# A fused attention and two mixture-of-experts layers on one core: x kept in weight slots, work reordered, products padded to fewer shapes

## The chip, the cores and the metric

One core of a Trainium2 chip. The time is the device time of one execution in microseconds; lower is better. Three executions are given with their median. A further execution was recorded by the profiler: its span runs from the first to the last instruction, and its own time is a little longer than the span.

## The reference, cut to what matters

Three layers run one after another. The attention has batch 4, 8 heads, 576 positions and 64 dimensions a head, and adds two parts.

```python
q_d, k_d, v_d = (z.reshape(B, H, S // 4, 4, D).mean(3) for z in (q, k, v))
out_up = repeat(softmax_attention(q_d, k_d, v_d), 4)     # pooled part
mask = abs(i - j) < 4                                    # banded part
x = out_up + softmax_attention(q, k, v, where=mask)      # then rows (2304, 512)

logits = x @ w_gate                                      # first expert layer
# the largest of all 2304 x 8 logits first: each token goes to one expert, each expert takes 288
out[mask_e] = relu(x[mask_e] @ w1[e]) @ w2[e]

logits = x @ phi                                         # second layer, 8 experts x 4 slots
d = softmax over tokens, c = softmax over slots
slot_out[e] = relu((d.T @ x)[e] @ m2w1[e]) @ m2w2[e]
out = c @ slot_out
```

## The kernel before, in words

The attention works in eight units, each two batches and two heads: the rows of a unit's arrays hold two heads, the columns two batches. Per unit the arrays loaded are k (64 rows x 1152 columns twice), q (128 x 1152), v (112 x 2304, cut into overlapping strips), and vp (128 x 1024 and 64 x 512, v grouped for pooling), all of 4 bytes, 2.87 MB. `load_k`, `load_q`, `load_v` and `load_p` (L68 to L89) issue them on SP; k, q and vp have two buffers, v has three.

Each step of a unit is a small function. For the banded part: `l_scores` (products of 32 queries with 38 keys, behind one product that writes the mask), `l_max`, `l_exp`, `l_norm`, `l_tr` (transposes on TensorE; ScalarE copies them into `aT`, and the ninth tile into `a8`), `l_av` (products with v; the ninth tile's contract 38 rows, the others 102). For the pooled part: `pool_k`, `pool_q`, `pool_v` on GpSimd, `d_scores`, `d_max`, `d_exp`, `d_norm`, `d_tr` (L220, transposes and small products of `e` and `e2`), `d_tr_out`, `d_av` (L252), `d_out`. `l_add` sums both into `xT`, x transposed; `l_x` (L305) transposes three row tiles at a time into `xu` (two buffers), and `l_st` (L322) stores a unit's 128 columns of x for nine row tiles into `x_dram` from ScalarE's queue: 0.59 MB in pieces of 512 bytes. `l_logit` adds the gate's logits.

The order is written out by hand. `FIRST` lists the steps before the first period, `UNIT0` those of period 0, `UNIT` those of the periods 1 to 8; an entry is a step and the unit relative to the period, so in period u the scores of unit u+1, the products with v of unit u and x of unit u-1 are made, and unit u+2 is loaded. Each engine, and SP's queue too, takes its instructions in this order.

Weights come through `Stream` (WS, L862): 1 MB slots, loads in the order of `todo` as slots come free. Nine slots `a0` to `a8` are there from the start. The entry `pump` loads one slot in each of the periods 2 to 6 and all free ones in period 7, when three of the attention's buffers are handed over too. After the attention eight slots `b0` to `b7` follow. The first 16 loads are halves of w2 transposed; `PMaker` (L511) makes P, the product of phi with each half, 32 TensorE products each, and `turn` transposes a finished one on VectorE.

`gating` searches prices for the eight experts in five rounds: VectorE and ScalarE compare, TensorE counts, a transposed sum goes back. Two P products stand behind the start and behind each round, one behind the totals and three behind the verdict (L788), at the end of `dispatch`. When the verdict is known, all engines branch, and `moe` starts: its rows of x are gathered by three indirect DMAs (`first_gather`), issued as soon as the indices `idx` are there.

In `moe` each expert's tokens go through `x_t` (transposes), `split` (a weight tile into two parts), `hidden` (12 products of 288 columns), `relu`, `h_rows`, the second layer's logits and weighted sums; lists give the order (`START`, `PERIOD`, `END`, `LAST`). `FINISH` lists the second layer: `first` and `second` are its products, `gathered` collects the slots' outputs, `combine` makes and stores the result. `weighted` (L1297) sums into four PSUM tiles, for the last expert named m, l, h and t; l is also read by `soft_lt`.

Of the kernel before, what the change touches and what calls it, by code (L numbers as in the profile page):

```python
# [36 lines left out]
def attention(nc, tc, ctx, kv, q, k, v, vp, C, x_dram, logit_tok, wg, pump):  # L37
# [145 lines left out]
    def d_exp(u):  # L183
# [3 lines left out]
        s["e2"] = e2 = sb.tile([64, SD, 2], F32, name="e2")  # L187
# [4 lines left out]
        for h in range(2):  # L192
            nc.scalar.activation(e2[:, :, h], p[0:64, h, 2], AF.Exp, bias=mx[0:64, h, 2:3], scale=1.0 / 128,
                                 accum_out=sm[0:64, h, 2:3])
        nc.scalar.activation(small(u, 24, 30), sm.rearrange("p h g -> p (h g)"), AF.Identity, bias=C["eps4"], scale=4.0)

    def d_norm(u):
        s = st[u]
        r = small(u, 24, 30)
        nc.vector.reciprocal(r, r)  # L200
        r = r.rearrange("p (h g) -> p g h", h=2)
        for bi in range(2):
            nc.vector.tensor_mul(s["e"][:, bi], s["e"][:, bi], r[:, bi, None, :].to_broadcast([128, SD, 2]))
        nc.vector.tensor_mul(s["e2"], s["e2"], r[0:64, 2, None, :].to_broadcast([64, SD, 2]))

    def l_tr(u, g):
        s = st[u]
        if g == 2:
            s["a8"] = sb.tile([128, 128], F32, name="a8")
# [3 lines left out]
        n = (3, 3, 2)[g]  # L213
        for r in range(2):
            sl = slice(64 * r, 64 * r + W)
            nc.scalar.activation(aT[sl, 3 * g:3 * g + n, :, r], p[sl, 0:n].rearrange("p s (c q) -> p s c q", c=4), AF.Copy)  # L216
        if g == 2:
            nc.scalar.activation(s["a8"][0:64 + W], p[0:64 + W, 2], AF.Copy)

    def d_tr(u):  # L220
# [6 lines left out]
        for h in range(2):  # L227
            nc.tensor.transpose(p[0:PD, 1, 64 * h:64 * h + 64], e2[:, 0:PD, h], ident[0:64, 0:64])
# [5 lines left out]
        for bi in range(2):  # L234
            for h in range(2):
                o, sl = slice(PR * h, PR * h + PR), slice(PR * bi, PR * bi + PR)
                c = 128 + SD * bi
                nc.tensor.matmul(p[o, 1, c + PD:c + SD], e2[:, PD:SD, h], ident[0:2 * PR, sl], start=True, stop=True,
# [13 lines left out]
    def d_av(u):  # L252
        s = st[u]
        od = tpsum([128, 2, SD])
        for bi in range(2):
            for part in range(2):
                for h in range(2):
# [3 lines left out]
                    nc.tensor.matmul(od[64 * h:64 * h + 64, bi], w, m, start=part == 0, stop=part == 1, skip_group_check=True)  # L261
# [12 lines left out]
    def l_av(u):  # L274
# [10 lines left out]
        for c in range(4):  # L285
            for h in range(2):
                rows = slice(64 * h, 64 * h + W)
                nc.tensor.matmul(p8[64 * h:64 * h + 64, QB * c:QB * c + QB], rows_v(s, rows, 8, c), s["a8"][rows, QB * c:QB * c + QB],
# [16 lines left out]
    def l_x(u, g):  # L305
        s = st[u]
        xT = s["xT"].rearrange("d b s -> d (b s)").rearrange("d (t i) -> d t i", i=128)
        p = tpsum([128, 3, 128])
        for i in range(3):
            nc.tensor.transpose(p[:, i], xT[:, 3 * g + i], ident)  # L310
        if g == 0:
            s["xu"] = sb.tile([128, 9, 128], F32, name="xu")
        nc.scalar.activation(s["xu"][:, 3 * g:3 * g + 3], p, AF.Copy)  # L313
# [20 lines left out]
    stages = dict(load_k=load_k, load_q=load_q, load_v=load_v, load_p=load_p, pool_k=pool_k, pool_q=pool_q, pool_v=pool_v,  # L334
# [23 lines left out]
    load_p(0)  # L358
    load_v(0)
# [6 lines left out]
    for t in dsm_b:  # L366
        nc.vector.memset(t, 1.0)
    edges(1)
# [10 lines left out]
FIRST = [  # L379
    ("load_k", 1),  # L380
    ("pool_k", 0, 0),
    ("load_q", 1),
    ("pool_k", 0, 1),
    ("pool_q", 0),
    ("d_scores", 0),
    ("d_max", 0),
    ("load_p", 1),
    ("d_exp", 0),
    ("l_scores", 0),
    ("load_v", 1),  # L390
    ("l_max", 0),
    ("d_norm", 0),
    ("pool_k", 1, 0),
    ("l_exp", 0),
    ("d_tr", 0),
    ("d_tr_out", 0),
    ("load_k", 2),
    ("pool_v", 0),
    ("pool_k", 1, 1),
    ("l_norm", 0),  # L400
    ("load_q", 2),
    ("l_scores", 1),
]
UNIT0 = [
    ("l_tr", 0, 0),
    ("l_tr", 0, 1),
    ("load_v", 2),
    ("pool_q", 1),
    ("d_av", 0),
    ("load_p", 2),  # L410
    ("d_out", 0),
    ("l_max", 1),
    ("d_scores", 1),
    ("d_max", 1),
    ("pool_v", 1),
    ("l_exp", 1),
    ("l_norm", 1),
    ("d_exp", 1),
    ("l_tr", 0, 2),
    ("d_norm", 1),  # L420
    ("l_av", 0),
    ("pump", 0),
    ("d_tr", 1),
    ("l_add", 0),
    ("pool_q", 2),
    ("l_x", 0, 0),
]
UNIT = [
    ("d_tr_out", 0),
    ("load_k", 2),  # L430
    ("pool_k", 1, 0),
    ("pool_k", 1, 1),
    ("load_q", 2),
    ("l_scores", 1),
    ("d_av", 0),
    ("l_tr", 0, 0),
    ("l_max", 1),
    ("load_v", 2),
    ("l_logit", -1),
    ("l_tr", 0, 1),  # L440
    ("l_exp", 1),
    ("d_scores", 1),
    ("l_tr", 0, 2),
    ("d_out", 0),
    ("d_max", 1),
    ("d_exp", 1),
    ("l_av", 0),
    ("l_add", 0),
    ("l_x", -1, 1),
    ("d_norm", 1),  # L450
    ("pool_v", 1),
    ("pool_q", 2),
    ("load_p", 2),
    ("l_x", 0, 0),
    ("l_x", -1, 2),
    ("l_norm", 1),
    ("l_lg", -1),
    ("l_st", -1),
    ("d_tr", 1),
    ("pump", 0),  # L460
# [50 lines left out]
class PMaker:  # L511
# [18 lines left out]
    def products(self, psum):  # L530
        self.product(psum)
        self.product(psum)

# [49 lines left out]
def gating(nc, tc, ctx, L, C, Z, idx, fill, first, force=None):  # L583
# [10 lines left out]
    def psum(shape):  # L594
        return ps.tile(shape, F32, name="t", bufs=4)
# [15 lines left out]
    fill.products(psum)  # L611
# [44 lines left out]
    def rounds(n, start=False):  # L656
        for r in range(n):
# [12 lines left out]
            fill.turn()  # L670
            fill.turn()
# [970 lines left out]
```

## Time and profile before

| | |
|---|---|
| three executions | 424.38, 428.37, 428.44 us, median 428.37 |
| profiled execution | 427.75 us, span 426.0 us |
| mean granted clock of TensorE | 0.917 |
| busy: TensorE, VectorE, ScalarE, GpSimd | 360.7, 235.9, 180.5, 127.4 us |
| moved by DMA | 122.52 MB, mean 288 GB/s |

Times in rows are microseconds from the span's start unless marked ns. PE is TensorE, DVE VectorE, ACT ScalarE, POOL GpSimd, SP the queue that issues most DMAs. A row of a timeline gives start, length from the first start to the last end, engine, line, operation, output and input by their names in the program, shapes and count, and in brackets the idle time ahead of it and who ended it. One product of 32-bit numbers shows as two records, a transpose as one. Idle time of an engine that does not bind costs nothing; a wait for several others is put down to the one that came last.

### The profile page before, as it was taken

To read this page: it belongs to the slowest core of one execution; us is meant where nothing else is said; L and a number is where in the kernel's file an instruction comes from. 1 tells how busy PE (TensorE), PEld (TensorE's weight loads), DVE (VectorE), ACT (ScalarE), POOL (GpSimd) and SP (SyncE) were. 2 spreads that over 40 slices of the span, in tenths; PEclk is the share of its full clock that TensorE was granted. 3 is DMA by queue.
4 is the path that set the end of the run, shared out by engine and by line. 5 is a ranking of instruction groups with operands and counts; after the bars stand their busy time and mean duration, and the time that the engine had idled before them with its cause. 6 is when DMAs were issued, how large, how long until landed. Compare 5 with 4: busy or idle time off the path is not lost. (4 is left out here: it accounts for less than half of the span.)

```text
span 426.0 us, 12313 instructions
## 1 busy us (share of the span) xinstructions
PE 360.7 (85%) x5116; PEld 270.1 (63%) x5116; DVE 235.9 (55%) x636; ACT 180.5 (42%) x497; POOL 127.4 (30%) x167
## 2 busy tenths in 40 slices
PE   0779989899559876757899999999999898689994
PEld 0456666666328556656878787887879685233693
DVE  4653647645505189763456676665758475424253
ACT  6362765567135434103545454453636343101231
POOL 6466663725340000042205050505141102240000
PEclk9885999989855899966999999999999999989997
DMA  8999978798997798934485999999997696989965
GB/s 230 274 268 246 205 201 274 226 291 264 260 397 275 226 382 310 425 109 161 157 295 195 329 333 335 353 360 323 363 321 254 230 390 267 373 320 411 408 244 217
DMA packets 31962, 122.52 MB, mean 288 GB/s; under 512 B 3232, under 2 KB 13088, under 8 KB 22688
## 3 DMA queue, kind: packets, MB, share of 16 engines
q1 hardware_dynamic: 19968, 111.85, 76.7%
q10 hardware_dynamic: 9632, 4.85, 4.1%
q0 software_dynamic: 2304, 5.02, 4.0%
q8 instruction: 41, 0.67, 0.7%
q14 instruction: 17, 0.14, 0.1%
HBM read 111.97 MB, written 9.73 MB: 286 GB/s over the span
## 5 line engine op out<-in xcount | busy, mean ns | idle before, releaser
L1293 POOL DMA_INDIRECT lg_rows<-lt,idx x24 | 24.6, 1026 | 114.0 <-DVE lt L1274 109.1
L1211 PE MATMUL h<-V,wh 128*128 128x288 f32 x128 | 37.9, 317 | 2.3 <-ACT V L1188 1.1
L1211 PE MATMUL t<-V,wh 128*128 128x288 f32 x128 | 37.9, 318 | 1.6 <-ACT wh L1196 1.6
L1212 PE MATMUL h<-V,wh 128*128 128x288 f32 x128 | 36.5, 306 | 0.5 <-DVE a L887 0.5
L1212 PE MATMUL t<-V,wh 128*128 128x288 f32 x128 | 35.0, 296 | 0.0
L216 ACT ACTIVATE aT<-t 38x384 f32<-38x384 f32 (+1 forms) x48 | 21.5, 448 | 26.4 <-PE t L212 25.6
L1198 DVE TENSOR_TENSOR wl<-b,wh 128x512 fp32r<-128x512 f32 x32 | 21.7, 682 | 18.7 <-ACT wh L1196 18.5
L1211 PEld LDWEIGHTS t<-V,wh 128*128 128x128 f32 x128 | 24.1, 188 | 8.5 <-issue 5.7
L1226 DVE STREAM_TRANSPOSE V<-hT 128x288 f32<-128x288 f32 x64 | 27.1, 453 | 4.1 <-issue 4.1
L1211 PEld LDWEIGHTS h<-V,wh 128*128 128x128 f32 x128 | 25.1, 196 | 6.4 <-issue 2.8
L1198 DVE TENSOR_TENSOR wl<-a,wh 128x512 fp32r<-128x512 f32 x32 | 21.7, 678 | 11.2 <-ACT wh L1196 10.7
L180 DVE TENSOR_REDUCE lg<-D 128x6 f32<-128x864 f32 x8 | 8.5, 1067 | 34.6 <-PE D L172 34.6
L1196 ACT ACTIVATE wh<-b 128x512 fp32r<-128x512 f32 x32 | 20.0, 631 | 16.4 <-DVEq L851 10.5
L1175 POOL DMA_INDIRECT kT<-x_dram,idx x21 | 20.2, 963 | 21.0 <-PE t L1186 17.0
L1212 PEld LDWEIGHTS h<-V,wh 128*128 128x128 f32 x128 | 25.2, 197 | 0.8 <-DVE a L887 0.8
L1220 ACT ACTIVATE hT<-h 128x288 f32<-128x288 f32 x32 | 13.1, 409 | 29.7 <-PE m L1243 15.3
L1212 PEld LDWEIGHTS t<-V,wh 128*128 128x128 f32 x128 | 24.1, 189 | 0.1
L1196 ACT ACTIVATE wh<-a 128x512 fp32r<-128x512 f32 x32 | 20.3, 633 | 8.5 <-PE h L1212 5.0
L282 PE MATMUL S<-aT,V 102*64 102x64 f32 x512 | 19.4, 239 | 5.0 <-ACT aT L216 2.9
L1214 PE MATMUL h<-V,wl 128*128 128x288 f32 x128 | 22.8, 301 | 0.0
L313 ACT ACTIVATE xu<-t 128x384 f32<-128x384 f32 x24 | 10.8, 485 | 27.9 <-DMA x_dram<-xu 17.4
L282 PEld LDWEIGHTS S<-aT,V 102*64 102x64 f32 x512 | 17.9, 152 | 7.3 <-ACT aT L216 3.1
(310 smaller groups left out, 963.5 us busy)
## 6 DMA issues: line engine op xcount, KB each, us to landing
a<-in_moe_w_dram SPq DMA_DIRECT2D x27, 1024.0 KB, 7.8
b<-in_moe_w_dram SPq DMA_DIRECT2D x21, 1024.0 KB, 12.1
a<-in_moe_w2t_dram SPq DMA_DIRECT2D x9, 1024.0 KB, 8.7
V<-in_v_dram SPq DMA_DIRECT2D x8, 1008.0 KB, 12.8
kT<-in_k_dram SPq DMA_DIRECT2D x16, 288.0 KB, 11.5
qT<-in_q_dram SPq DMA_DIRECT2D x8, 576.0 KB, 12.8
x_dram<-xu ACTq DMA_DIRECT2D x8, 576.0 KB, 13.7
vp<-in_vp_dram SPq DMA_DIRECT2D x8, 512.0 KB, 13.6
```

The costliest lines, as they stand in the source:

```text
L216: nc.scalar.activation(aT[sl, 3 * g:3 * g + n, :, r], p[sl, 0:n].rearrange("p s (c q) -> p s c q", c=4), AF.Copy)
L282: nc.tensor.matmul(p[64 * h:64 * h + 64, k // 2, o:o + 64], rows_v(s, slice(0, 64 + W), 2 * k + h, c), aT[0:64 + W, 2 * k + h, c].rearrang ...
L313: nc.scalar.activation(s["xu"][:, 3 * g:3 * g + 3], p, AF.Copy)
L1175: nc.gpsimd.indirect_dma_start(out=xs[0:96, DM * c:DM * c + DM], out_offset=None, in_=x_dram, in_offset=bass.IndirectOffsetOnAxis(ap=idx[: ...
L1196: nc.scalar.activation(wh, w, AF.Copy)
L1198: nc.vector.tensor_sub(wl, w, wh.bitcast(F32))
L1211: nc.tensor.matmul(p, wh[:, dt], xh[:, dt], start=dt == 0, stop=False)
L1212: nc.tensor.matmul(p, wh[:, dt], xl[:, dt], start=False, stop=False)
L1214: nc.tensor.matmul(p, wl[:, dt], xh[:, dt], start=False, stop=dt == 3)
L1220: nc.scalar.activation(h, st.pop(("ph", e, ft)), AF.Relu)
L1226: nc.vector.transpose(st["hb", e][:, :, ft], st.pop(("hr", e, ft)).rearrange("p (b t) -> p b t", t=32))
L1293: nc.gpsimd.indirect_dma_start(out=lg_rows[3 * e + c], out_offset=bass.IndirectOffsetOnAxis(ap=idx[:, 3 * e + c:3 * e + c + 1], axis=0), i ...
```

## The change

Eight parts.

1. x stays on the chip for four units: `l_x` makes 4 + 4 + 1 row tiles and writes them into slots `a5` to `a8` (and a small tile), and `l_st` stores all 512 columns once after units 3 and 7, from SP. `Stream` starts with five slots; `a5` and `a6` join in period 7, `a7` and `a8` behind the `b` slots.
2. Products: the ninth tile of l_av contracts 102 rows from `aT`; `e2` has 128 rows with zeros, its transposes become products of 128 rows; d_av makes its 32-row products first and its 112-row ones after.
3. `FIRST`, `UNIT0` and `UNIT` are reordered: unit 0's scores ahead of its pooled part, its vp and v loaded later.
4. `warm` products, which write a tile that nobody reads, in `FIRST`: 10, 10 and 16 of 256 bf16 columns.
5. P: three products at the gate's start, one in the last round, four behind the totals, none behind the verdict; finished ones are transposed in the rounds and behind the verdict.
6. `moe` starts with 8 + 2 + 2 warm products of 512 columns around `x_t`; `LAST` has 10.
7. `weighted` of the last expert writes m, h, h, t.
8. `FINISH`: `first_t` and, near the end, `second` and `gathered` stand earlier.

```diff
@@ attention
-    aT = one.tile([128, 8, 4, 2, QB], F32, name="aT")
+    aT = one.tile([128, 9, 4, 2, QB], F32, name="aT")
+    e2_b = [one.tile([128, SD, 2], F32, name=f"e2{i}") for i in range(2)]
...
     def l_tr(u, g):
-        if g == 2:
-            s["a8"] = sb.tile([128, 128], F32, name="a8")
...
-            nc.scalar.activation(aT[sl, 3 * g:3 * g + n, :, r], p[sl, 0:n].rearrange("p s (c q) -> p s c q", c=4), AF.Copy)
-        if g == 2:
-            nc.scalar.activation(s["a8"][0:64 + W], p[0:64 + W, 2], AF.Copy)
+            nc.scalar.activation(aT[sl, 3 * g:3 * g + 3, :, r], p[sl].rearrange("p s (c q) -> p s c q", c=4), AF.Copy)
     def d_tr(u):
...
-            nc.tensor.transpose(p[0:PD, 1, 64 * h:64 * h + 64], e2[:, 0:PD, h], ident[0:64, 0:64])
+            nc.tensor.matmul(p[0:PD, 1, 64 * h:64 * h + 64], e2[:, 0:PD, h], ident[:, 0:64], start=True, stop=True,
+                             skip_group_check=True)
...
     def d_av(u):
-        for bi in range(2):
-            for part in range(2):
+        for part in (1, 0):
+            for bi in range(2):
...
     def l_av(u):
-                rows = slice(64 * h, 64 * h + W)
-                nc.tensor.matmul(p8[...], rows_v(s, rows, 8, c), s["a8"][rows, QB * c:QB * c + QB],
+                nc.tensor.matmul(p8[...], rows_v(s, slice(0, 64 + W), 8, c), aT[0:64 + W, 8, c, h],
...
     def l_x(u, g):
+        n = (4, 4, 1)[g]
+        p = tpsum([128, n, 128])
+        for i in range(n):
+            nc.tensor.transpose(p[:, i], xT[:, 4 * g + i], ident)
+        if hp == 0:
+            if g < 2:
+                x = wa.tile([128, 2048], F32, name=f"a{5 + 2 * pr + g}").rearrange("p (t d) -> p t d", d=DM)
+            else:
+                x = sb.tile([128, 1, DM], F32, name="xu8")
+            st["xu", pr, g] = x
+        nc.scalar.activation(st["xu", pr, g][:, :, 128 * hp:128 * hp + 128], p, AF.Copy)
...
     def l_st(u):
-        nc.scalar.dma_start(x_dram.rearrange("(p j) d -> p j d", j=NT)[:, 9 * pr:9 * pr + 9, 128 * hp:128 * hp + 128],
-                          st.pop(u)["xu"])
+        if hp == 3:
+            for g in range(3):
+                n = (4, 4, 1)[g]
+                nc.sync.dma_start(rows[:, 9 * pr + 4 * g:9 * pr + 4 * g + n], st.pop(("xu", pr, g)))
...
+    def warm(u, n):
+        w = ident.bitcast(BF16)
+        p = tpsum([128, 256])
+        for _ in range(n):
+            nc.tensor.matmul(p, w[:, 0:128], w[:, 0:256], start=True, stop=True)
@@ gating
-    fill.products(psum)
+    for _ in range(3):
+        fill.product(psum)
...
-            fill.turn()
-            fill.turn()
+            while fill.made:
+                fill.turn()
...
-            fill.products(psum)
+            for _ in range(1 if start and r == n - 1 else 2):
+                fill.product(psum)
@@ dispatch
         zs, inc = totals()
+        if what is not None:
+            for _ in range(4):
+                fill.product(psum)
...
-            for _ in range(3):
-                fill.product(psum)
-            for _ in range(3):
+            while fill.made:
                 fill.turn()
@@ moe, fused
-        names = "m", "l", "g" if e < E - 1 else "h", "t"
+        names = ("m", "l", "g", "t") if e < E - 1 else ("m", "h", "h", "t")
...
+            warm(e, 8)
...
+                if e == -1 and name == "x_t" and args[0] < 2:
+                    warm(e, 2)
...
-    WS.free = [(wa, f"a{i}") for i in range(9)]
+    WS.free = [(wa, f"a{i}") for i in range(5)]
...
-                WS.free += [(kv, x) for x in ("V2", "kT1", "V0")]
+                WS.free += [(wa, "a5"), (wa, "a6")] + [(kv, x) for x in ("V2", "kT1", "V0")]
...
         WS.add_slots(wb, [f"b{i}" for i in range(8)])
+        WS.add_slots(wa, ["a7", "a8"])
```

The lists before and after, cut to their loads, x and the steps next to them: `UNIT` before ends with `l_x 0 0`, `l_x -1 2`, `l_norm 1`, `l_lg -1`, `l_st -1`, `d_tr 1`, `pump 0`; after, with `l_x 0 0`, `pump 0`, `l_lg -1`, `l_x -1 2`, `pool_v 1`, `l_norm 1`, `d_tr 1`, `l_st -1`, `pool_q 2`. `FIRST` before begins with the loads k, q, vp, v of unit 0 and k 1, q 1, vp 1, v 1; after, with k 0, q 0, vp 0, k 1, q 1, v 0, vp 1, v 1.

## Rows read from the trace of the kernel before

**Rows 1.** Windows: stretch, length, busy time (instructions) per engine, granted clock, DMA share, GB/s
```profile
4.00:60.00 56.00, 42.24 (x689) 29.32 (x689) 28.14 (x59) 29.66 (x87) 35.12 (x37) 0.85 1.03 254
60.00:100.00 40.00, 35.58 (x669) 25.22 (x669) 24.82 (x55) 23.31 (x81) 20.86 (x27) 0.96 0.77 238
113.00:137.00 24.00, 17.26 (x213) 12.57 (x202) 6.59 (x14) 9.75 (x31) 9.09 (x13) 0.51 0.89 315
195.20:202.00 6.80, 5.62 (x22) 5.30 (x23) 2.43 (x6) 1.59 (x4) 2.37 (x3) 0.50 0.70 241
225.00:325.00 100.00, 100.00 (x1212) 80.99 (x1212) 66.32 (x179) 49.13 (x121) 29.84 (x30) 1.00 0.96 328
```
**Rows 2.** Timeline of DVE: the gate's first reduction, and the totals
```profile
150.43 0.30 DVE L600 TENSOR_REDUCE mm<-L 128x1 f32<-128x144 f32 x1
...
179.39 0.46 DVE L702 TENSOR_TENSOR_SCAN dinc<-g,Dl 128x144 f32<-128x144 f32 x1 [1.11 <-PE g L698]
```
**Rows 3.** Who waited for whom: us in total, times, longest
```profile
ACT xu L313 <- DMA x_dram<-xu: 17.4, 3, 11.8
```
**Rows 4.** The same of SP's queue, 40 to 125 us
```profile
SPq L88 <- DMA x_dram<-xu: 11.6, 1, 11.6
```
**Rows 5.** Timeline of PE in one steady unit
```profile
67.23 0.47 PE L126 MATMUL S<-mask,identb 128*128 128x380 bf16 x2
67.63 1.39 PE L131 MATMUL S<-kT,qT 128*32 128x76 f32 x72
68.95 0.47 PE L261 MATMUL t<-eT,Vd 112*64 112x144 f32 x4
...
70.53 0.54 PE L212 MATMUL t<-ident,sc 128*102 128x128 f32 x3
...
74.04 2.08 PE L282 MATMUL S<-aT,V 102*64 102x64 f32 x64 [0.35 <-ACT sc L151]
76.05 0.66 PE L288 MATMUL t<-a,V 38*64 38x32 f32 x16
...
80.78 1.45 PE L131 MATMUL S<-kT,qT 128*32 128x76 f32 x72
```
**Rows 6.** Timeline of PE and ACT, 112 to 120 us: unit 7 and x
```profile
112.76 2.09 PE L131 MATMUL S<-kT,qT 128*32 128x76 f32 x72 [2.30 <-DMA qT<-in_q_dram]
...
119.47 0.87 ACT L313 ACTIVATE xu<-t 128x384 f32<-128x384 f32 x2 [11.77 <-DMA x_dram<-xu]
```
**Rows 7.** Timeline of PE behind the verdict, 186 to 203 us
```profile
187.03 5.11 PE L525 MATMUL t<-b,phi 128*32 128x128 f32 x94
193.59 1.18 PE L1186 MATMUL t<-ident,kT 96*128 96x96 f32 x12 [1.45 <-DVEq L851]
195.92 0.61 PE L1211 MATMUL h<-V,wh 128*128 128x288 f32 x1 [1.14 <-ACT V L1188]
...
202.39 0.29 PE L1211 MATMUL t<-V,wh 128*128 128x288 f32 x1
```
**Rows 8.** The chain that ended last: start, us, what
```profile
375.03 12.20 PE h L1427 x96
...
388.57 3.64 PE h L1427 x32
...
416.77 0.60 ACT kT L1167
...
418.43 0.65 PE h L1479 x4
```
**Rows 9.** Timeline of PE, 38 to 41 us: the third unit's scores
```profile
38.86 2.38 PE L131 MATMUL S<-kT,qT 128*32 128x76 f32 x68
```
**Rows 10.** Timeline of POOL: the third gather
```profile
189.39 0.92 POOL L1146 DMA_INDIRECT kT<-x_dram,idx  x1 [0.30 <-remote]
```
**Rows 11.** DMA issues, 186 to 193.5 us: count, median us to landing
```profile
kT<-x_dram,idx POOLq DMA_INDIRECT x3, 3.5
```
**Rows 12.** Timeline of PE in the last weighted sum
```profile
366.62 0.37 PE L1309 MATMUL l<-V,dT 32*32 32x256 f32 x1 [0.94 <-DVE lt L1274]
```

More of the change, by code (lines that the diff above doesn't have):

```diff
@@ L260, in d_av @@
                     w, m = (s["Vd"][0:PD, g], s["eT"][0:PD, bi, h]) if part == 0 else (s["Vd"][r, 4 + bi], s["eR"][r, bi])
[L261 removed]
+                    nc.tensor.matmul(od[64 * h:64 * h + 64, bi], w, m, start=part == 1 and bi == 0, stop=part == 0, skip_group_check=True)
         s["od"] = od
@@ L305, in l_x @@
     def l_x(u, g):
[L306 to L313, printed above, removed]
+        pr, hp = divmod(u, 4)
+        xT = st[u]["xT"].rearrange("d b s -> d (b s)").rearrange("d (t i) -> d t i", i=128)
+        n = (4, 4, 1)[g]
[9 more added lines that the diff above has]
+        nc.scalar.activation(st["xu", pr, g][:, :, 128 * hp:128 * hp + 128], p, AF.Copy)
     def l_logit(u):
@@ L367, in attention @@
         nc.vector.memset(t, 1.0)
+    for t in e2_b:
+        nc.vector.memset(t[64:128], 0.0)
     edges(1)
@@ L594, in psum @@
     def psum(shape):
-        return ps.tile(shape, F32, name="t", bufs=4)
+        return ps.tile(shape, F32, name="t", bufs=5)
     mm = one.tile([128, 2], F32, name="mm")
@@ L749, in dispatch @@
             nc.vector.tensor_reduce(slot[:, h], sl[:, h], axis=AX.X, op=ALU.add)
-        if what is not None:
-            fill.turn()
-            fill.turn()
-            fill.product(psum)
         ci = sb.tile([128, NT], I32, name="dci", bufs=1)
@@ L787, in dispatch @@
         if what is not None:
-            for _ in range(3):
-                fill.product(psum)
-            for _ in range(3):
+            while fill.made:
                 fill.turn()
@@ L959 @@
     ("second", 3, 0),
+    ("second", 3, 1),
     ("combine", 2, 1),
-    ("second", 3, 1),
-    ("combine", 2, 0),
     ("gathered", 3, 0),
     ("gathered", 3, 1),
+    ("combine", 2, 0),
     ("combine", 3, 0),
@@ L1341, in slots_acc, with warm @@
             nc.vector.scalar_tensor_tensor(acc, acc, cor[e % 2], p, op0=ALU.mult, op1=ALU.add)
-    def psum(shape):
-        return ps.tile(shape, F32, name="t", bufs=3)
-    stages = dict(hidden=hidden, relu=relu, split=split, x_t=x_t, gather=gather, h_rows=h_rows,
+    def warm(e, n):
+        w = ident.bitcast(BF16)
+        p = ps.tile([128, 2, 256], F32, name="t", bufs=3)
+        for _ in range(n):
+            nc.tensor.matmul(p, w[:, 0:128], w[:, None, :].to_broadcast([128, 2, 256]), start=True, stop=True)
+    stages = dict(warm=warm, hidden=hidden, relu=relu, split=split, x_t=x_t, gather=gather, h_rows=h_rows,
                   logits2=logits2, logits2_out=logits2_out, soft=soft, soft_exp=soft_exp, soft_d=soft_d, soft_lt=soft_lt, scatter=scatter, weighted=weighted, weighted_out=weighted_out, weighted_sum=weighted_sum,
```

128 lines of the change are left out of this document (66 added, 62 removed).

## The prediction, made before the changed kernel ran

> **What bounds the kernel now.** I read stages first, by busy time and granted clock in windows. From 225 to 325 us TensorE is busy 100.00 of 100.00 us at full clock [rows 1]: the expert stage is bound by TensorE's products, and the change leaves its products and their order alone. So I look before and behind it.
>
> The attention (0 to 150.43, where the gate's first reduction starts on VectorE [rows 2]) is not like that. From 4 to 60 us the DMA engines are full (share 1.03) and bring 254 GB/s; from 60 to 100 the share is 0.77 and the rate 238 [rows 1]. The reader should see a full queue that then has holes, although loads are still due. Two views of waits say what makes them. ScalarE waits 17.4 us, three times, for the store of x out of `xu` [rows 3], because `xu` has two buffers and a unit's store must have landed before the next but one is evacuated. And SP stands 11.6 us before it issues a load of `vp`, released by the landing of such a store [rows 4]; that load uses nothing of x, so the two can only share a semaphore that the later transfer must find free. A store lands late because it goes out in 512-byte pieces behind megabytes of loads, and the loads behind it are late in turn.
>
> The price shows in one unit. A steady unit takes 13.15 us, from one unit's banded scores at 67.63 to the next's at 80.78 [rows 5]. Unit 7's scores wait for its q until 112.76, and ScalarE stands 11.77 us before 119.47 for the store [rows 6]; from 113 to 137 the clock is at 0.51 of full, that is, at the lower of its two levels, 1.2 and not 2.4 GHz [rows 1]. From 112.76 to the end of the attention it takes 37.7 us.
>
> Behind the gate, three of the P products run on TensorE from 187.03 for 5.11 us after the verdict, and the expert stage starts at 193.59, its first hidden product at 195.92, with the clock at 0.50 from 195.2 to 202 [rows 1, 7]. At the end, the first product of the second stage takes 12.20 us for 96 records where 32 take 3.64 [rows 8].
>
> **The change part by part. x in weight slots.** The eight ScalarE stores go; in their place stand two sets of three stores on SP, after units 3 and 7, of 4 + 4 + 1 row tiles, 2.36 MB a set, in runs of 8 KB (2 KB for the single tile). ScalarE's evacuations write 1152 columns a unit either way (3 x 384, or 512 + 512 + 128). So the 17.4 us on ScalarE and the stores' hold on SP go. What is late next? The loads. A unit loads 2.87 MB (the four arrays in the code), 11.3 us at 254 GB/s. Up to q of unit 7 the queue carries 7 x 2.87 + 1.18 = 21.3 MB, three weight slots (3.15 MB) and half of x (2.36 MB), before and after alike. So that q lands earlier by what the queue idled: 23% of the 40 us from 60 to 100, 9.2 us [rows 1]. 112.76 - 9 = 104. That is also the order of the compute: the third unit's scores start at 38.86 [rows 9]. The new first list puts k and q of unit 1 ahead of v of unit 0 (1.03 MB, 4.1 us at 254 GB/s) and scores ahead of the pooled part, so I take 4 us off that (0 to 7), and five periods of 12.8 follow: 35 + 64 = 99, under the 104 of the data. The data decide.
>
> From unit 7's scores to the end I take one steady period less the savings below, 12.6, and a last one without scores and without the next unit's pooled part, about 10.5: 23 at full clock. Part of it will be at the lower clock after the wait; the scores' 72 records took 2.09 us there against 1.39 [rows 5, 6], so I take 25 (23 to 30). End of the attention 104 + 25 = 129 against 150.4: **-21.4** (bounds -27 with the data at 100 and full clock, -12 with the data at 108 and 30 us behind).
>
> What pays for it: weights have five slots instead of nine until unit 7, so two more megabytes of the transposed w2 follow the attention, behind 2.36 MB of x on SP: six w2t halves, 6.3 MB, and x are 8.7 MB, 34 us even at 254 GB/s if all started at the end of the attention. The products of the last four halves stand behind the gate's five rounds, 29 us on (VectorE takes up their totals at 179.39, and started at 150.43 [rows 2]). At 328 GB/s [rows 1] it is 26 us and they are there; at 254 they would hold the dispatch 5 to 6 us. I take 0 and keep the 6 for the range. The second x store must land before the first gather, some 35 us later: hidden.
>
> **Warm products in the first list.** 36 products of 256 bf16 columns. Nearest row: two bf16 products of 380 and 304 columns take 0.40 us from 67.23 to 67.63 [rows 5], so 0.15 each, 5.4 us in all at full clock and twice that at the lower. They stand where TensorE waits for VectorE and for the data (q of unit 2 is behind seven megabytes). I take them as hidden; unhidden they eat the 4 us above.
>
> **Fewer shapes.** The pooled products d_av alternate between 112-row and 32-row weights, 16 records in 1.58 us (68.95 to 70.53); the 64 records of l_av, all of one shape, take 2.01 us (74.04 to 76.05), 0.031 each, while the 16 of 38 rows are busy 0.66, 0.041 each [rows 5]. At l_av's pace d_av's records of 144 columns would take 16 x 0.031 x 144/64 = 1.1 us, so its four changes of shape cost about 0.1 us each, an estimate. Two fewer there and one each in l_av and d_tr: 0.4 us a unit, 3 us over eight units if TensorE bounds them, nothing where data do. It is inside the 12.8 and 12.6. The Trainium skill speaks against the padding: "TensorEngine Tiling (Array Packing)", Theoretical Speedup, gives products of up to 64 contracted rows up to twofold speed as independent tiles, which 102 rows give up; by it the sum would be that of rival 4, 404. The rows have the wide records cheaper (0.031 against 0.041), and I go by them.
>
> **Gate.** Three products instead of two at its start and one fewer in its last round: beside VectorE's work, 0 (-1 to +1). The three after the verdict move to the wait behind the totals: 5.11 us of TensorE leave the branch. But the first hidden product also needs three gathers; the third is issued at 189.39 and the landing takes 3.5 us [rows 7, 10, 11]: about 192.9. One transpose and its two evacuations take some 0.7, so 193.6 instead of 195.92: -2.3. From there to 202.39 two hidden groups ran in 6.47 us at half clock [rows 1, 7]; at full they take 3.2: -3.2. The fill (8 + 2 + 2 products of 512 columns, 0.3 us each by the same row, 3.6 us in all) must sit inside the wait for the gathers, or it eats part. Of 5.5 I take **-4.5** (0 to -6).
>
> **End.** The last weighted product no longer writes the tile that VectorE still transposes: 0.94 us of wait [rows 12], -0.9. Fill keeps the clock: 12.20 - 3 x 3.64 = 1.3 us, I take -1.1 [rows 8]. Moving the last `gathered` ahead of a `combine` covers the 1.66 us from 416.77 to 418.43 where the chain leaves TensorE [rows 8]: -1.2. Sum **-3.2** (0 to -3.9).
>
> **Sum.** -21.4 - 4.5 - 3.2 = -29.1 from the profiled execution's own 427.75 us (span 426.0): 398.7. The median of the three is 428.37, 0.6 above, so on that scale nothing changes.
>
> **The rivals.**
> 1. *The wait moves to SP.* SP is in order: the first x store waits there for unit 3's last evacuation and stands ahead of all loads of unit 7, its 2.36 MB another 9.3 us at 254 GB/s. For it: k of unit 7 can't be issued before that point anyway, so they queue up. Against: the same bytes were carried before. Then q lands at 113 again, the end is 138 (-12.4), and the time 427.75 - 12.4 - 4.5 - 3.2 = 407.7.
> 2. *Loads at 254 GB/s and a low clock.* The queue stays as slow as from 4 to 60 us [rows 1], the low clock follows the wait, w2t holds the dispatch: end 137, +6 at the dispatch, half of the rest: 427.75 - 13.4 + 6 - 4 = 416.4.
> 3. *Slower: the low clock all through the attention.* TensorE waits for data in every unit, and a unit costs 1.5 times as much (2.09 against 1.39 [rows 5, 6]): 12.6 becomes 18.9. From 35, five periods end at 129.5, then 18.9 and 15: 163, +13, and 427.75 + 13 - 3.2 = 437.5. Each low period costs 6.3 us; it turns the sign from the fifth on (29.1 / 6.3). For it: 24 us at 0.51 after one wait. Against: 60 to 100 us at 0.96 [rows 1].
> 4. *The padded products lose by their width.* The 16 records of 38 rows lie in two row ranges, h by h; wide ones would have to follow each other and take twice the 0.66 us [rows 5]: 0.66 a unit, 5.3 over eight, 404.0. For it only the rule named above; against it the 0.031 of rows 5.
>
> **How the numbers follow.** Forecast 0.60 (own range 390 to 406), rival 1 0.22, rival 2 0.11, rival 3 0.05, rival 4 0.02. All but the third, and a small part of the second with worse luck, are faster by over 1%, which is about what a measurement of this kernel tells from no change: 0.93, 0.03 within it, 0.04 slower. The range takes in the attention's better bound with the other terms nearly whole, 388, and rival 2: 416.
>
> **What would show it.** Right: no ScalarE wait for x, no SP wait for a store in a `vp` load, DMA share near 1 from 60 to 100 us, unit 7's scores near 104 and waiting for q, the gate's first reduction near 129; the first hidden product some 43 us after it (45.5 now) and at full clock; the first product of the second stage near 11 us. Wrong: scores of unit 7 near 113, or reached late without a data wait; products of the gate waiting for a DMA; fill products in the chain of waits.

## The result and the profile after

The changed kernel takes 412.77 us (median of four, 409.87 to 415.23) against 428.40 for the kernel before in the same rounds: a ratio of 0.965 with an interval of 0.956 to 0.974, that is 15.6 us. Forecast was 29. The profiled execution took 415.23 us (span 413.5), so against its own counterpart 12.5 us went. The stages of the two profiled executions, in us:

| | before | after | difference | forecast |
|---|---|---|---|---|
| start to unit 7's scores | 112.76 | 120.48 | +7.7 | -8.8 |
| to the gate's first reduction | 37.7 | 24.6 | -13.0 | -12.7 |
| to the indices of the gathers | 35.8 | 35.1 | -0.7 | 0 |
| to the first hidden product | 9.7 | 9.9 | +0.2 | -2.3 |
| first two hidden groups | 6.5 | 3.7 | -2.7 | -3.2 (I took 4.5 of the 5.5) |
| to the first product of the second layer | 172.6 | 171.3 | -1.4 | -0.9 |
| to the end of the span | 51.0 | 48.4 | -2.5 | -2.3 |

All but the first row came out within 2.5 us of its forecast. The first was wrong in sign, by 16.5 us. These are the windows of the kernel after, in the columns of [rows 1] (the last three: granted clock, DMA share, GB/s):

```profile
4.00:60.00 56.00, 42.46 (x725) 31.88 (x726) 27.91 (x60) 30.32 (x85) 32.72 (x40) 0.94 1.03 229
60.00:100.00 40.00, 34.78 (x568) 29.48 (x568) 21.99 (x46) 21.67 (x72) 18.07 (x19) 0.79 1.03 236
120.50:144.50 24.00, 21.63 (x367) 16.56 (x368) 9.99 (x21) 13.09 (x38) 9.35 (x13) 0.93 0.76 301
190.00:196.50 6.50, 6.27 (x45) 6.06 (x46) 2.75 (x6) 2.49 (x5) 0.92 (x1) 1.00 0.72 224
```

The holes in the DMA engines' time are gone from 60 to 100 us, as forecast (1.03 for 0.77). But the rate did not follow: 236 GB/s where it was 238 with the holes, and from 4 to 60 us it fell from 254 to 229. The clock behind unit 7's scores and at the expert stage's start is high now (0.93 and 1.00, for 0.51 and 0.50).

The page's list of DMA issues (count, size of one, median us from issue to landing) shows the same from the other side:

```profile
V<-in_v_dram SPq DMA_DIRECT2D x8, 1008.0 KB, 20.7
...
kT<-in_k_dram SPq DMA_DIRECT2D x16, 288.0 KB, 16.7
qT<-in_q_dram SPq DMA_DIRECT2D x8, 576.0 KB, 17.8
vp<-in_vp_dram SPq DMA_DIRECT2D x8, 512.0 KB, 19.5
```

Before, these were 12.8, 11.5, 12.8 and 13.6. More is under way at once, and each load takes longer: counted every 5 us from 30 to 85 us, 7 to 9 loads that SP had issued had not landed yet; before it was 2 to 7. The waits of ScalarE up to 145 us no longer hold the 17.4 us for a store [rows 3]; what ScalarE waits for in the evacuation of x is TensorE alone:

```profile
ACT a L314 <- PE t L307: 14.1, 9, 3.4
```

The wait moved to SP. In its timeline nothing but the store of x stands between a weight load at 89.30 us and k of unit 7 at 101.35; the first piece of x waits 4.4 us for an earlier load of a weight slot to land, the second and third for unit 3's last evacuations, and q comes behind them:

```profile
89.30 0.49 SPq L901 DMA_DIRECT2D a<-in_moe_w2t_dram  x1
94.26 6.07 SPq L330 DMA_DIRECT2D x_dram<-a  x2
100.93 0.32 SPq L330 DMA_DIRECT2D x_dram<-xu  x1
101.35 3.17 SPq L74 DMA_DIRECT2D kT<-in_k_dram  x2
105.16 0.34 SPq L79 DMA_DIRECT2D qT<-in_q_dram  x1
```

Now TensorE's timeline in the attention: the scores of units 2 to 7 (L132), products with V (L279), and the stalls that no data explains ("issue"):

```profile
37.01 1.39 PE L132 MATMUL S<-kT,qT 128*32 128x76 f32 x72 [1.87 <-DMA qT<-in_q_dram]
...
45.60 2.08 PE L279 MATMUL S<-aT,V 102*64 102x64 f32 x64
...
52.43 1.39 PE L132 MATMUL S<-kT,qT 128*32 128x76 f32 x72
...
60.78 0.44 PE L173 MATMUL D<-kd,qd 64*32 64x144 f32 x4 [3.09 <-issue]
...
61.62 3.13 PE L279 MATMUL S<-aT,V 102*64 102x64 f32 x64
...
70.20 1.39 PE L132 MATMUL S<-kT,qT 128*32 128x76 f32 x72
...
78.65 1.61 PE L279 MATMUL S<-aT,V 102*64 102x64 f32 x37 [1.92 <-issue]
...
87.00 1.39 PE L132 MATMUL S<-kT,qT 128*32 128x76 f32 x72
...
95.76 1.74 PE L279 MATMUL S<-aT,V 102*64 102x64 f32 x38 [1.70 <-issue]
...
103.68 0.82 PE L132 MATMUL S<-kT,qT 128*32 128x76 f32 x34 [0.71 <-issue]
...
120.48 2.51 PE L132 MATMUL S<-kT,qT 128*32 128x76 f32 x72 [4.45 <-DMA qT<-in_q_dram]
```

The periods, from one unit's scores to the next's, are 15.4, 17.8, 16.8 and 15.1 us where I took 12.8. Between 50 and 110 us TensorE stands 7.4 us in four stalls in the middle of groups of products, and behind each of the first three the granted clock is at its lower level for a while: the 64 products with V take 3.13 us at 61.62 and 2.08 at 45.60. q of unit 7 costs only the last 4.45 us.

The first three of these stalls have something in common, which the DMA view of a narrow stretch shows. From 57.8 to 59.2, from 75.9 to 77.2 and from 92.6 to 94.2 us one packet of 16 KB of the queue called instruction is on its way; this is the row of the first stretch (packets, MB, share):

```profile
q8 instruction: 1, 0.02, 5.8%
```

There are 42 such packets in the whole span. The trace gives their ends as 59.19, 77.20 and 94.18: each stall ends 1.4 to 1.6 us later, and the fourth (103.68) 1.5 us after a packet that ends at 102.19. Not every packet is followed by a stall. Where "issue" stands ahead of the first product of a group, as before d_av, it can be a data wait that the profile does not name; only stalls in the middle of a group are counted here.

Where the stalls stand in TensorE's own order says more. Counted in its product records from the start of the execution, the four come behind 725, 977, 1230 and 1357 records. In the fourteen traces of this case (the kernel before, the one after, and the twelve runs below) there are 53 such stalls of over 0.3 us between 20 and 150 us, and each comes behind 472, 599, 725, 851, 977, 1104, 1230, 1357, 1483 or 1610 records (one or two fewer in e12, whose products differ), at whatever time that is. Behind 725 records, for example, stand the stalls at 60.78 above, at 58.23 in e11, the changed kernel again, and at 62.01 in the kernel before, whose order is another:

```profile
58.23 0.44 PE L173 MATMUL D<-kd,qd 64*32 64x144 f32 x4 [2.22 <-issue]
```

```profile
62.01 1.04 PE L282 MATMUL S<-aT,V 102*64 102x64 f32 x28 [0.74 <-issue]
```

These places lie 126 or 127 records apart; TensorE's 5190 product records make 41 such stretches, and there are 42 packets. So a stall stands where TensorE passes from one packet's worth of its instructions to the next, whatever data is due there.

A note on what follows. The runs were made in three sessions, on chips that the record numbers 0, 6 and 0: the kernel before took 454.3 us beside e1 to e4, 457.3 beside e5 to e8, and 425.2 beside e9 to e12. In the traces of the first two sessions the stretch from the first hidden product to the second layer takes 202 to 210 us for 175 here; why is not known. So runs are compared by their ratio to the kernel before in the same session, and by stages of the attention. Some runs of e2, e5 and e6 were disturbed, the profiled ones of e2 and e6 among them, so no ratio is given for these three.

### The profile page after: what moved, and what is told of

It reads as the page before. It is cut to its first block, busy times and chain, and to the rows that moved or that the text cites. A ratio compares the mean times of both kernels' runs of the same rounds, so it can differ in the third digit from the quotient of the medians.

```text
span 413.5 us, 12436 instructions
## 1 busy us (share of the span) xinstructions
PE 358.8 (87%) x5190; PEld 275.9 (67%) x5190; DVE 237.4 (57%) x638; ACT 181.2 (44%) x489; POOL 126.3 (31%) x167
## 5 line engine op out<-in xcount | busy, mean ns | idle before, releaser
L1225 PE MATMUL h<-V,wh 128*128 128x288 f32 x128 | 36.4, 306 | 1.7 <-ACT wh L1210 1.1
L214 ACT ACTIVATE aT<-t 38x384 f32<-38x384 f32 x48 | 23.2, 484 | 31.0 <-PE t L211 30.5
L1226 PE MATMUL h<-V,wh 128*128 128x288 f32 x128 | 35.0, 296 | 0.2 <-DVE a L897 0.2
L1212 DVE TENSOR_TENSOR wl<-a,wh 128x512 fp32r<-128x512 f32 x36 | 24.5, 681 | 15.5 <-ACT wh L1210 15.1
L1225 PEld LDWEIGHTS h<-V,wh 128*128 128x128 f32 x128 | 24.0, 188 | 5.9 <-issue 2.8
L1210 ACT ACTIVATE wh<-a 128x512 fp32r<-128x512 f32 x36 | 22.8, 633 | 10.6 <-PE h L1226 7.6
L279 PE MATMUL S<-aT,V 102*64 102x64 f32 x512 | 19.8, 240 | 7.4 <-issue 3.6
L1189 POOL DMA_INDIRECT kT<-x_dram,idx x21 | 19.9, 945 | 18.8 <-PE t L1200 15.1
L1234 ACT ACTIVATE hT<-h 128x288 f32<-128x288 f32 x32 | 13.1, 409 | 26.9 <-PE m L1257 15.3
L279 PEld LDWEIGHTS S<-aT,V 102*64 102x64 f32 x512 | 18.2, 152 | 9.6 <-ACT sc L152 4.9
L1226 PEld LDWEIGHTS h<-V,wh 128*128 128x128 f32 x128 | 24.1, 188 | 0.4 <-DVE a L897 0.4
L132 PE MATMUL S<-kT,qT 128*32 128x76 f32 x576 | 13.7, 256 | 12.2 <-DMA qT<-in_q_dram 10.0
L295 DVE TENSOR_TENSOR xT<-S,up 128x512 f32<-128x512 f32 x16 | 10.3, 684 | 21.5 <-PE S L279 21.5
L1212 DVE TENSOR_TENSOR wl<-b,wh 128x512 fp32r<-128x512 f32 x24 | 16.1, 679 | 11.1 <-ACT wh L1210 10.6
L1228 PE MATMUL t<-V,wl 128*128 128x288 f32 x128 | 22.2, 295 | 0.0
## 6 DMA issues: line engine op xcount, KB each, us to landing
b<-in_moe_w_dram SPq DMA_DIRECT2D x21, 1024.0 KB, 12.5
V<-in_v_dram SPq DMA_DIRECT2D x8, 1008.0 KB, 20.7
kT<-in_k_dram SPq DMA_DIRECT2D x16, 288.0 KB, 16.7
qT<-in_q_dram SPq DMA_DIRECT2D x8, 576.0 KB, 17.8
```

The lines of the kernel that those rows point to most:

```text
L132: nc.tensor.matmul(o[QB * c:QB * c + QB], qT[:, bi, QB * j:QB * j + QB], kT[:, :, 13 + S * bi + QB * j:13 + S * bi + QB * j + W], start=Fa ...
L214: nc.scalar.activation(aT[sl, 3 * g:3 * g + 3, :, r], p[sl].rearrange("p s (c q) -> p s c q", c=4), AF.Copy)
L279: nc.tensor.matmul(p[64 * h:64 * h + 64, k // 2, o:o + 64], rows_v(s, slice(0, 64 + W), 2 * k + h, c), aT[0:64 + W, 2 * k + h, c].rearrang ...
L1189: nc.gpsimd.indirect_dma_start(out=xs[0:96, DM * c:DM * c + DM], out_offset=None, in_=x_dram, in_offset=bass.IndirectOffsetOnAxis(ap=idx[: ...
L1210: nc.scalar.activation(wh, w, AF.Copy)
L1212: nc.vector.tensor_sub(wl, w, wh.bitcast(F32))
```

## The experiments

Theories: A, the bytes ahead of q of unit 7 and their order on SP set the end of the attention; B, TensorE is held by its own instructions, which come late while much is under way, and by the low clock behind such stalls; C, the rate of the loads alone.

**e1, x stored behind unit 7's loads.** `l_sx` stores x of units 0 to 3; `l_st` then stores only x of units 4 to 7.

```diff
     ("load_p", 2),
+    ("l_sx", -2),
     ("l_x", -1, 1),
```

> The changed kernel with one thing moved: the store of x of units 0 to 3 goes out behind the loads of unit 7 instead of ahead of them. Theory A (order on SP: q of unit 7 is late because SP first waits for unit 3's last evacuation and then sends 2.36 MB of x): q lands some 10 us earlier (2.36 MB at 237 GB/s), at about 110 instead of 120.35. TensorE has the mask product of unit 7 done at 116.0, so the scores come at 116 at most 4.5 us earlier, and at the full clock; gate at 139 to 140, time 406 to 408. Theory B (TensorE is held by stalls that no data explains, those that the trace calls issue, not by data): the scores of unit 7 come no more than 4.5 us earlier as well, but the periods of units 2 to 6 stay at 14 to 18 us. Theory C (the rate of the loads alone sets the end): q lands at 115 or later, nothing won, 412.

Ratio 0.970 (0.963 to 0.978). SP issues q of unit 7 at 89.2 us instead of 105.2, and TensorE waits for no load any more; unit 7's scores start at 114.9. But the stalls are 9.1 us between 20 and 150 us, the periods 13.2 to 19.0, and the gate starts at 141.0 where the changed kernel's three profiled runs (here, e5, e11) have 145.1, 134.4 and 138.5. So A is right about the wait and wrong about its worth: behind it stood B.

**e2, V in two buffers.**

```diff
-        s["kT"], s["sc"], s["V"] = kT_b[u % 2], sc_b[u % 2], V_b[u % 3]
+        s["kT"], s["sc"], s["V"] = kT_b[u % 2], sc_b[u % 2], V_b[u % 2]
```

> The changed kernel with two buffers for V instead of three: V of unit u+2 can be issued only when the products with V of unit u are done, so about 1 MB less is under way at any time; the bytes and their order are the same. Theory B (TensorE's own instructions come late, because their fetches, 16 KB packets on queue 8, stand behind what is under way; the four stalls between 57 and 104 us are 7.4 us, each ends some 1.5 us after such a packet, and the low clock follows them): the stalls fall below 3 us, periods of units 2 to 6 come to 13 to 14 us, time 404 to 409. Theory C (rate of the loads): landing times as before or later, time 412 to 416. If the queue runs empty while SP waits: share under 0.95 and 415 or more.

In this order the load of V of unit u+2 stands ahead of the products of unit u, which so read the V of the later unit and wait for it: the run computes something else. It took 453.46 us against 454.3 and tells nothing on B; e7 is what was meant.

**e3, three weight loads later.**

```diff
-            WS.pump((0, 0, 1, 1, 1, 1, 1, None)[u])
+            WS.pump((0, 0, 0, 0, 0, 1, 1, None)[u])
```

> The changed kernel with the three weight loads that stand ahead of q of unit 7 (3.15 MB, periods 2 to 4) left to period 7; two stay in periods 5 and 6. Theory A and C (bytes ahead of q7): q lands 13 us earlier (3.15 MB at 237 GB/s), about 107, and the scores at 112 to 116; what is won is given back in part where the gate's products wait for the transposed w2: 406 to 413. Theory B: as many loads are under way at any time (eight), so the stalls stay at 6 us or more and the scores come at 114 or later.

Ratio 0.963 (0.954 to 0.971); unit 7's scores at 108.4, gate at 134.6, no product of the gate waits for a DMA. While the share was 1.03 (25 to 75 us) the periods were 16.9, 15.3 and 15.8; from 75 to 100 us it fell to 0.78, and the periods to 13.2 and 12.9, with no stall behind 75.98 us until the next scores:

```profile
50.00:75.00 25.00, 19.95 (x385) 14.44 (x385) 15.94 (x30) 13.14 (x40) 18.61 (x27) 1.00 1.03 242
75.00:100.00 25.00, 22.46 (x450) 17.43 (x451) 15.67 (x34) 14.98 (x51) 11.06 (x10) 1.00 0.78 229
```

Both theories had the scores too late (112 to 116, and 114 or later), and B its 6 us of stalls: there were 5.5 from 50 to 110 us. The shorter periods fit B better than A, which has no reason for them. And here the clock stayed full through stalls of 2.5, 1.4 and 1.1 us, so the stalls alone make the difference: less them, the periods of 15.3 and 15.8 are 12.8 and 13.3.

**e4, x stored per unit again.** `l_x`, `l_st` and the nine slots as before, all else as changed:

```diff
-                nc.sync.dma_start(rows[:, 9 * pr + 4 * g:9 * pr + 4 * g + n], st.pop(("xu", pr, g)))
+        nc.scalar.dma_start(x_dram.rearrange(...)[:, 9 * pr:9 * pr + 9, 128 * hp:128 * hp + 128], st.pop(u)["xu"])
```

> The changed kernel with its first part undone: x evacuated by thirds into xu and stored per unit from ScalarE's queue, nine slots from the start; the rest (order, products, fill) as changed. Theory: the 13.0 us won between unit 7's scores and the gate (37.7 to 24.6 us) come from x in slots, since ScalarE no longer waits for a store; undone, ScalarE waits 12 to 17 us for xu again, that stretch is 33 us or more, and the time is 418 to 424. Rival (the new order and the products with fewer shapes did it): the stretch stays under 28 us and the time is 412 or less.

Ratio 1.008 (0.996 to 1.021): with the store as before, everything else of the change together brings nothing. What x in slots brings without the rest was not run. The wait is back, longer than the 12 to 17 us expected, and the gate starts at 160.1, 39.2 us behind unit 7's scores at 120.9:

```profile
ACT xu L309 <- DMA x_dram<-xu: 27.4, 2, 14.9
```

**e5 and e6, the changed kernel again, and e1 and e3 together.**

> The changed kernel itself, as the measure for the other three on the same chip. Expected: 0.96 to 0.98 of the time of before; gate 5 us earlier than before; the periods of units 2 to 6 at 14 to 18 us, with 6 to 9 us of stalls called issue between 50 and 110 us, each ending 1.4 to 1.8 us after a 16 KB packet of queue 8.

> Both moves together: x of units 0 to 3 stored behind the loads of unit 7, and three weight loads left to period 7, so 5.5 MB fewer stand ahead of q of unit 7. Theory A (bytes ahead of q7, at 230 to 237 GB/s): q7 at 100 or earlier and no longer what TensorE waits for; with theory B (the stalls go when the queue is no longer full, as between 75 and 100 us of the run with the weights later, where the periods were 13.2 and 12.8) the scores of unit 7 at 105 to 109, gate at 129 to 134, that is 11 to 16 us ahead of the changed kernel, and 8 to 14 us off its time. If the transposed w2 is late, products of the gate wait for a DMA and 3 to 8 us of that are lost again. If the stalls do not depend on the queue: scores at 113 or later, 3 to 5 us won.

Medians 443.87 (430.2 to 448.6) and 435.72 (427.4 to 438.1). The profiled run of e5 was its fastest: its loads came at 316 GB/s from 75 to 100 us, nothing waited for q of unit 7, and its gate started at 134.4; still TensorE had 5.9 us of stalls up to 110 us and periods of 12.9 to 19.2. e6 loaded at 217 to 228 GB/s from 25 to 100 us at a share of 1.00 to 1.03, and did not wait for q of unit 7 either; but it had 7.7 us of stalls from 50 to 110 us, unit 7's scores at 113.2 and its gate at 136.3. That is what was written for stalls that do not depend on the queue (113 or later), not the 105 to 109 of theory B. But the queue was as full as before; so e6 shows that fewer bytes ahead of q do not help by themselves.

**e7, V in two buffers, in order.** As e2, and `load_v` of unit u+2 moved behind `l_av` of unit u.

> V in two buffers, its load moved behind the products that read the buffer before (in the earlier run with two buffers it stood ahead of them, so those products read the V of a later unit). About 1 MB less under way at any time, same bytes. Theory B: stalls under 4 us between 50 and 110 us instead of 6 to 9, periods of 13 to 14.5, scores of unit 7 4 to 8 us earlier than in the changed kernel unless its q holds them. Theory C (the rate of the loads alone): the landings of q at the same times or later, since SP now waits, and nothing won.

Ratio 0.973 (0.969 to 0.977). TensorE's waits from 50 to 112 us hold one stall left of the 5.9 (e5) to 7.4 us (here):

```profile
PE D L173 <- issue: 1.3, 1, 1.3
```

The periods are 13.3, 14.1, 14.7, 15.5. But SP waits for its buffers (share 0.74 from 25 to 50 us), so q of unit 7 is late:

```profile
114.24 2.51 PE L132 MATMUL S<-kT,qT 128*32 128x76 f32 x72 [6.66 <-DMA qT<-in_q_dram]
```

So both theories hold, one behind the other: fewer bytes under way take the stalls away, and then the bytes ahead of q7 bind. None of e1, e3, e7 and e8 is told apart from the changed kernel's 0.965 by its time; what they show is in the stages.

**e8, no fill before the experts.**

```diff
-            warm(e, 8)
...
-                if e == -1 and name == "x_t" and args[0] < 2:
-                    warm(e, 2)
```

> The changed kernel without the 8 + 2 + 2 products that write nothing anybody reads, around the first transposes of the expert stage. Theory (the fill runs past the landing of the first gather, 184.72, to 186.5, and delays the transposes): from the indices to the first hidden product 8.2 to 8.8 us instead of 9.85; but the clock is then at its lower level for the first 6 us of hidden products, 2.7 to 3.2 us from there to the gather of the third expert. Net 1 to 2.5 us slower than the changed kernel. Rival (the branch and the gathers hold the first product, the fill lies in their wait): 9.7 us as before, and 2.7 to 3.2 us slower.

Ratio 0.968 (0.951 to 0.984). The first hidden product comes 8.4 us behind the indices, the third group 5.1 us after that:

```profile
181.13 0.61 PE L1225 MATMUL h<-V,wh 128*128 128x288 f32 x1 [0.58 <-issue]
...
186.25 0.29 PE L1225 MATMUL t<-V,wh 128*128 128x288 f32 x1
```

In the changed kernel, timeline of TensorE with the fill (L1362) and the transposes (L1200):

```profile
182.93 3.57 PE L1362 MATMUL t<-ident 128*128 128x512 bf16 x8 [1.79 <-PEq L861]
186.30 0.84 PE L1200 MATMUL t<-ident,kT 96*128 96x96 f32 x4
...
190.03 0.40 PE L1225 MATMUL h<-V,wh 128*128 128x288 f32 x1 [0.58 <-ACT V L1202]
...
193.78 0.29 PE L1225 MATMUL t<-V,wh 128*128 128x288 f32 x1
```

The first gather had landed at 184.72, and the first transpose waited for the fill to end. From the indices to the third group it is 13.5 us without fill, 13.6 with it here, 12.7 in e5, and 12.7 to 13.7 in the other runs with the whole fill and no late gather: the fill buys the clock with what it delays, and is worth nothing to 0.8 us. Of the 1 to 2.5 us that I expected to lose without it at most 0.8 shows. Of the 16.2 us before, the change's gain of 2.6 is there without the fill.

**e9 to e12, on one chip.** e9 is e1, e3 and e7 together; e10 the same with 5 + 1 + 1 products of fill; e11 the changed kernel; e12 the changed kernel with the products of its second part as before.

> Three moves together: V in two buffers with its load behind the products that read the buffer before, x of units 0 to 3 stored behind the loads of unit 7, three weight loads left to period 7. Theory (two limits: TensorE's late instructions while about 5 MB are under way, and the bytes ahead of q of unit 7): the stalls stay at 1 to 2 us between 50 and 110 us as with V in two buffers alone, and q7, with 5.5 MB fewer ahead of it, lands before TensorE is there; periods 13 to 14, scores of unit 7 at 103 to 107, gate at 127 to 131, and 4 to 10 us off the time of the changed kernel on this chip. If only the bytes counted: gate at 134 to 137 as with the two moves alone. If SP's waits starve TensorE: scores of units 3 to 6 wait for q, gate at 135 or later.

> The run before with 5 + 1 + 1 instead of 8 + 2 + 2 products of fill at the start of the expert stage. Theory (what the fill costs is its length beyond the landing of the first gather): from the indices to the first hidden product 8.7 to 9.3 us instead of 9.0 to 9.9, hidden products at full clock still (second group 1.50 us behind the first, not 2.20), 0.3 to 1 us less in all. Rival: 5 products are too few, the clock stays low, and the groups come as without fill.

> The changed kernel once more, as the measure for the other three on the same chip: 0.95 to 0.98 of before, gate between 134 and 145 us by how fast the loads come.

> The changed kernel with the second part undone: the ninth tile of l_av contracts 38 rows again, e2 has 64 rows and is transposed, d_av takes its products pair by pair. Theory (fewer shapes cost TensorE less: 1.28 us from the first product of d_av to the next step instead of 1.58, ninth tile 0.54 instead of 0.58, d_tr 1.87 instead of 1.84): undone, a unit is 0.3 us longer on TensorE, gate 0 to 3 us later, too little to see in the times. Rival 4 of the prediction (wide products lose): undone, the unit is 0.3 to 0.7 us shorter.

| | median | ratio | unit 7's scores | gate | to indices | to hidden |
|---|---|---|---|---|---|---|
| e9 | 406.73 | 0.958 (0.954 to 0.962) | 102.2 | 125.3 | 35.7 | 15.0 |
| e10 | 405.98 | 0.955 (0.951 to 0.959) | 106.5 | 129.6 | 36.2 | 14.5 |
| e11 | 408.98 | 0.964 (0.959 to 0.969) | 113.6 | 138.5 | 34.7 | 10.0 |
| e12 | 412.43 | 0.967 (0.959 to 0.975) | 113.3 | 139.4 | 35.1 | 9.6 |

The windows of e9, and then of e11, from 50 to 100 us (clock, share and GB/s at the end):

```profile
50.00:75.00 25.00, 22.09 (x410) 16.72 (x412) 17.58 (x35) 16.95 (x56) 15.97 (x23) 1.00 0.79 205
75.00:100.00 25.00, 21.52 (x438) 16.20 (x427) 14.43 (x32) 16.65 (x55) 14.16 (x14) 1.00 0.78 200
```

```profile
50.00:75.00 25.00, 20.69 (x384) 15.46 (x381) 13.40 (x30) 14.25 (x43) 15.73 (x23) 0.93 1.03 244
75.00:100.00 25.00, 21.24 (x330) 18.24 (x331) 12.81 (x29) 12.02 (x42) 15.97 (x16) 0.80 1.03 267
```

e9 moves fewer bytes per second, has a share of 0.79 and a full clock, and is 13 us ahead at the gate; counted as above, 1 to 6 of its loads are under way. Its periods are 13.2, 13.3, 13.9, 13.4 and 14.2 (e11: 13.2, 16.4, 16.2, 17.3, 12.9), its stalls up to 100 us 2.2 us (e11: 6.4). Of the 13 us 4.4 arrive at the end of the span. Most of the loss, 5.0 us, lies between the indices and the first hidden product, because the weights left for later now stand ahead of the gathers (five loads of 1 MB under way when the first gather is issued, two in e11); 1.0 goes before that, and 2.7 behind it, 1.6 of them in the first two hidden groups. In e9's timeline TensorE waits for the first of them:

```profile
170.49 0.90 PE L1208 MATMUL t<-ident,kT 96*128 96x96 f32 x4 [3.49 <-DMA kT<-x_dram,idx]
```

That gather was issued at 161.52 and landed at 170.44, 8.9 us, where the changed kernel's takes 4.1. So the indices come 12.1 us earlier than in e11 and the first hidden product 7.1. e9 and e10 both come in ahead of the changed kernel, by 2.3 and 3.0 us in the medians; the six times of e10 all lie below the six of e11, those of e9 overlap with them a little. For e9 4 to 10 us were expected. e10 does not settle what the fill costs: TensorE waits for the gathers there, and the clock is low again when they come.

In e12 d_av takes the 1.58 us of before again; the changed one takes 1.28 (53.75 to 55.03, its two groups):

```profile
53.75 0.71 PE L258 MATMUL t<-eR,Vd 32*64 32x144 f32 x8
54.38 0.71 PE L258 MATMUL t<-eT,Vd 112*64 112x144 f32 x8
55.03 0.86 PE L211 MATMUL t<-ident,sc 128*102 128x128 f32 x6
```

The ninth tile takes 0.54 for 0.58 and d_tr 1.87 for 1.84, in all 0.3 us a unit. In the times e12 and e11 can't be told apart.

## Why the prediction was right and where it was wrong

**Right:** faster, and mainly by x in weight slots (without it the rest brings nothing, e4). From unit 7's scores to the gate I took 25 us, it is 24.6 (24.9 in e11), because ScalarE waits for no store and the clock stays up. The second layer's start and the end gave 3.9 us for the 3.2 forecast. The fill in the first list is hidden: unit 2's scores wait 1.87 us for q and for nothing else.

**Luck:** 412.8 lies above the forecast's own range of 390 to 406, between rival 1's 407.7 and rival 2's 416.4, and so in the outer range only because that reached to rival 2. The term for the attention, -21.4, was -5.3: its second half came as forecast, its first with the wrong sign.

**Wrong, the first term:** "that q lands earlier by what the queue idled". The share of busy time was taken for capacity. At 0.77 the engines brought 238 GB/s, at 1.03 236: with more loads under way each one takes longer, and the idle share was no reserve. q of unit 7 was there at 120.35 us, not at 104. In e11, with faster loads, it was there at 112.07.

**Wrong, the second term, and the one that decides:** "five periods of 12.8 follow". I took the period from the best unit of the trace [rows 5], 13.15 us at a share of 0.77 to 0.87. The five periods of the kernel before from unit 2's scores (38.86) to unit 7's (112.76) were 14.4, 14.4, 13.2, 16.3 and 15.7; with the queue full they are 15 to 18 here. Even if q had been there at 104, TensorE was not ready for it before 116.0, and in e1, e5 and e11, where it did not wait for q, unit 7's scores came at 114.9, 109.7 and 113.6 for the 99 I had. What was left out is the stalls of TensorE and the low clock behind some of them: fewer bytes under way take most of both away (e7, e9), and then the periods are 13.3 to 15.5 and 13.2 to 14.2. In numbers: from unit 2's scores to unit 7's the five periods took 83.5 us for the 64 I took. Of that 7.4 are stalls and 4.5 the wait for q, which leaves 71.6; e9 took 68.0, 65.8 without its stalls of 2.2. So 12.8 was short by 0.4 us a period, and the 5.8 between 71.6 and 65.8 I put down for the most part to the clock (0.79 from 60 to 100 us, in e9 1.00), an estimate. Nothing in the prediction looked at stalls; the trace of before has one in the middle of a group, 0.74 us at 62.01.

**Rivals.** The first came true in its mechanism (SP is held by the store of x from 90 to 101 us), but e1 shows that what stood behind it left of its price at most the wait of 4.45 us. The second had the rate nearly right (229 to 236 GB/s for 254), not the clock behind unit 7, and the dispatch was not held; its 416.4 lies nearest to what was measured, but by another way. The third, the low clock all through, happened in part: 0.79 from 60 to 100 us, behind stalls and not behind waits for data. The fourth fell: the wide products do not lose (0.54 for 0.58), so the rule of the Trainium skill quoted there ("TensorEngine Tiling (Array Packing)", Theoretical Speedup) does not show in this trace. Fewer shapes won 0.3 us a unit of the 0.4 estimated.

**The expert stage's start.** "-2.3" for the branch without P products was 1.3 (8.4 for 9.7, e8), and the fill ate it, as the prediction warned; the two hidden groups won 2.7 of 3.2. The gate won 0.7 where I had 0. Of the signs of being wrong that the prediction named, two came: unit 7's scores were late, and fill products held others up.

**Open:** that the 16 KB packets carry TensorE's instructions follows from the places of the stalls, one packet's worth apart in its order. That a packet comes late because other loads are under way is shown by e7 and e9 as far as the effect goes; how the packet is held up is not shown, nor why some places have a stall in one run and none in another. Nor is it shown what limits the attention's loads to 221 to 254 GB/s in most stretches and let 316 through in one of e5, while weights alone come at 412 (after, 150 to 175 us).

## What to carry to other kernels

Here a DMA share below 1 was not spare rate: before counting idle share as time, look whether stretches with a full queue move more bytes. When loads are made to queue without gaps, ask what else goes through the same engines, instruction packets and gathers among them; e9 is faster with a lower share. When an engine stops with no wait for data, count where it stops in its own order: the same places in every run point at its instructions. And take the period of a loop from the units whose conditions the change will bring, not from the best one.

## What the runs showed of the hardware

- TensorE can stand still in the middle of a group of products with all its data there: 0.3 to 3.5 us at a time, each ending 1.3 to 1.7 us after a 16 KB packet of the instruction queue, up to 9.1 us in one attention (e1). The 53 stalls of fourteen traces stand at ten fixed places of its order, 126 or 127 product records apart.
- The granted clock falls to its lower level behind some of these stalls (after, the first three) and not behind others (e3, full from 50 to 100 us through stalls of 1.1 to 2.5 us).
- The attention's loads take 11.5 to 13.6 us from issue to landing (medians) with the holes and 16.7 to 20.7 without, at no higher rate (238 and 236 GB/s from 60 to 100 us).
- An indirect gather that lands 4.1 us after its issue takes 8.9 when five loads of 1 MB are under way (e9).
- The kernel before took 425, 454 and 457 us in three sessions (medians); the record gives the first two of these the same chip number.
